# Attention and gated MLP on one core: the bias spread by a TensorE product, q of step 3 requested after W_spatial, and a new order up to the third W_spatial product

## The chip, the cores and the metric

One core of one Trainium2 chip runs the whole program. The metric is the device time of one execution in microseconds (us), and the median of several runs is what is compared. The engines are TensorE (PE, matrix products and transposes), VectorE (DVE), ScalarE (ACT), GpSimd (POOL) and SyncE (SP, which here only issues DMA requests). Each engine works through its own instructions in order and waits on semaphores for the others.

## The reference, cut to what matters

There are 4 batches of 768 tokens, 8 heads of 64 channels, and a hidden width of 1024. First comes causal linear attention with a decay per head, in blocks with a running state; the token-mixing gated MLP follows on its output.

```python
# attention, block by block of the sequence
intra = einsum('bhij,bhjd->bhid', einsum('bhic,bhjc->bhij', qb, kb) * Dmask, vb)
out[:, :, sl] = intra + einsum('bhid,bhde->bhie', qb * lam_pow, kv_state)
kv_state = lam_block * kv_state + einsum('bhsd,bhse->bhde', kb * rev_pow, vb)
# gated MLP on x = heads side by side, 512 wide
h = maximum(x @ w_in, 0);  u, v = h[..., :512], h[..., 512:]
v_n = (v - mean(v)) / sqrt(var(v) + 1e-06)
v_s = einsum('ts,bsd->btd', w_spatial, v_n) + b_spatial[None, :, None]
return (u * v_s) @ w_out
```

## The kernel before, in words

The work of one batch is three steps of 256 tokens, so there are twelve steps (0 to 11); after the three steps of a batch the spatial product and the output product of this batch follow. A step loads q, k and v (512 KB each, three buffers for each, filled in turn), multiplies q and k by decay factors, transposes both, forms the masked scores and the state, and leaves the attention output transposed in `xT`, from which the two halves of `x @ w_in` are formed.

The order of the work is written out by hand: `ORDER` is one string of tokens, read from left to right. A token is a step's name, its arguments, and the letter of the engine that runs it (T for PE, D for DVE, A for ACT, P for POOL, S for SP). Each engine runs its own tokens in the order of the string; semaphores put in by the framework let it wait for data of others and for a buffer or a PSUM bank to come free. Eight banks of PSUM are named by number as the last arguments of a token; bank 7 holds the attention state.

The names that matter here, with the line of the kernel that the profile shows:

- LQ, LK, LV (L192): load of q, k, v of a step, requested by SP. QM, KM (L280): the decay of q and k into `qc` and `kc`, in two halves. VC: v to bf16.
- TQ, TK (L310) and EQ, EK: transposes of q and k on PE and their copy out of PSUM. From step 5 on, DQ (L297) and DK (L293) do the same by a DMA transpose that SP requests.
- SC (L340): scores; MK (L345): scores times mask, on DVE; KV (L357): the state; SS: its copy to `s_sb`; AV (L378, L387): attention output in two halves, the second behind FN, a copy of one element that stands as a wait; EX: its copy to `xT`.
- WI (L243) and WS (L248): the requests for the halves of W_in and of W_spatial, issued by POOL, which converts to bf16 on the way. WO: W_out. BS (L255): the bias row, written by one DMA to all 128 partitions of `bsp`.
- PV (L412) and EV (L417, L419): the v half of `x @ w_in` and its relu; BN (L427, L428), RA (L432), RD (L437), RB (L442): mean and variance, square root, reciprocal, and the product of negated mean and reciprocal; VN (L451): the normalized v. PU (L463) and EU: the u half.
- WT (L475) and EW: transposes of W_spatial and their copies. GP: the bias into a PSUM bank; PW (L489): the W_spatial product added to it (six matmuls); GM (L495): times u. PO (L500), EO, ST: output product, copy and store.
- FL (L263): filler products of `ones` whose result nobody reads; `FL.6.256.4.0` is six of 256 columns into bank 4. GT (L239) and GN (L455): copies of one element on POOL that stand as waits, GT for a load to land, GN for a VN. tab: a load of ACT's function table.

Copies share the lines of a helper: L177 on ACT, L179 on DVE, L181 on POOL. All arguments of a token begin with the step (for GP, PW, GM, PO with the batch), so KM.3.1 is the second half of the decay of k of step 3.

Two buffers each stand behind `kc`, `qc`, `kT` and `qT`, so KM.5 can only run when KV.3.1, the last reader of step 3's `kc`, is done.

Of the kernel before, what the change touches and what calls it, by code (L numbers as in the profile page):

```python
# [562 lines left out]
```

## Time and profile before

| | us |
|---|---|
| median of 3 runs | 144.92 (144.47 to 144.94) |
| the profiled execution | 145.1 |
| its span from first to last instruction | 143.4 |
| PE busy in it | 134.0 |
| DVE busy | 111.9 |
| ACT busy | 75.9 |
| POOL busy | 57.2 |

The granted clock of PE is 1.0 over the whole execution. The profile's start is the span's start; a time in the text such as "at 19.64" is counted from there. Busy times are sums over instructions of one engine; matmuls overlap in the pipeline, so the time of a run of matmuls is best taken from the chain of waits, where each piece is counted once. A bracket at the end of a line of the timeline tells how long the engine was idle before the instruction and what ended that. Where a wait is for several things, the profile names the one that came last, and now and then it names a neighbour of it.

### The profile page before, as it was taken

The page shows a single profiled execution, that of the slowest core. Times are in us where ns is not written, and L with a number is a line of the kernel's source. Part 1 is how long each engine was busy: PE and PEld are TensorE (multiplying, and loading weights), DVE is VectorE, ACT ScalarE, POOL GpSimd, SP SyncE. Part 2 cuts the span into 40 slices and gives each one's busy share as a digit, 9 for nine tenths or more (in the row PEclk, how much of TensorE's full clock was granted, in tenths as well). Part 3 has the DMA queues.
Part 4 walks back from the last instruction along what each step waited for, and adds up shares of the span by engine and source line. Part 5 has one row for each costly group of instructions (what it writes and reads, how often), then busy time and mean ns, then how long its engine had stood idle before and what let it go on. Part 6 is the DMA issues. An engine that isn't in the chain of part 4 may idle for free.

```text
span 143.4 us, 4693 instructions
## 1 busy us (share of the span) xinstructions
PE 134.0 (93%) x1979; PEld 87.4 (61%) x1997; DVE 111.9 (78%) x222; ACT 75.9 (53%) x150; POOL 57.2 (40%) x65
## 2 busy tenths in 40 slices
PE   5998889999999999899999999999999999999990
PEld 3767655768566575566566455685664655855550
DVE  1489957899596988498999779968797989984940
ACT  3136725689726566749823567598227542580041
POOL 5657954296997514089513224603800000000000
PEclk9999999999999999999999999999999999999999
DMA  3999999999999989999989799799968251410075
GB/s 87 344 346 308 266 259 214 229 316 305 293 323 274 158 182 346 335 207 318 201 251 119 187 349 308 205 337 174 271 166 209 99 209 62 162 73 0 14 297 201
DMA packets 58374, 32.27 MB, mean 225 GB/s; under 512 B 15858, under 2 KB 55282, under 8 KB 58354
## 3 DMA queue, kind: packets, MB, share of 16 engines
q1 hardware_dynamic: 55968, 29.23, 76.8%
q0 software_dynamic: 2384, 2.75, 11.3%
q8 instruction: 15, 0.25, 0.6%
q14 instruction: 5, 0.04, 0.1%
q10 hardware_dynamic: 2, 0.00, 0.0%
HBM read 24.77 MB, written 6.29 MB: 217 GB/s over the span
## 4 chain that ended last, share of the span: by engine, by line
PE 70%; DVE 10%; DMA 5%; POOL 4%; ACT 4%; issue 2%; SPq 2%; DVEq 0%
PE ps L489 19%; PE ps L500 12%; PE ps L463 11%; PE ps L412 10%; DMA q_in<-in_q_dram 5%; PE ps L263 4%; POOL kc L280 3%; PE ps L310 3%; PE ps L340 3%; DVE a_sb L345 2%; PE ps L387 2%; PE ps L357 2%; PE ps L378 2%; SPq L293 1%; DVE wt_sb L179 1%
## 5 line engine op out<-in xcount | busy, mean ns | idle before, releaser
L489 PE MATMUL ps<-wt_sb,vn 128*128 128x384 bf16 x192 | 34.0, 327 | 0.0
L345 DVE TENSOR_TENSOR a_sb<-ps,m 128x1024 bf16<-128x1024 f32 x24 | 28.6, 1215 | 1.0 <-PE ps L340 0.6
L280 POOL TENSOR_TENSOR kc<-k_in,lv 128x512 bf16<-128x512 f32 x18 | 19.2, 1079 | 24.5 <-DMA k_in<-in_k_dram 12.1
L489 PEld LDWEIGHTS <-vn 128*128 128x128 bf16 x192 | 18.1, 98 | 12.3 <-ACT vn L448 0.4
L280 POOL TENSOR_TENSOR qc<-q_in,lqn 128x512 bf16<-128x512 f32 x19 | 20.5, 1092 | 7.7 <-DMA qT<-qc 2.8
L463 PE MATMUL ps<-xT,win_sb 128*128 128x256 bf16 x192 | 23.4, 273 | 0.0
L412 PE MATMUL ps<-win_sb,xT 128*128 128x512 bf16 x88 | 22.1, 380 | 0.6 <-DVE xT L179 0.2
L500 PE MATMUL ps<-wout_sb,gT 128*128 128x512 bf16 x82 | 21.1, 379 | 0.9 <-issue 0.6
L495 DVE TENSOR_TENSOR gT<-ps,uT 128x384 bf16<-128x384 f32 x32 | 16.8, 551 | 5.6 <-PE ps L489 4.9
L463 PEld LDWEIGHTS <-win_sb 128*128 128x128 bf16 x192 | 18.2, 98 | 3.9
L427 DVE BATCH_NORM_STATS2 st<-vh 128x6 f32<-128x512 bf16 x24 | 16.4, 682 | 1.1 <-ACT vh L417 0.7
L417 ACT ACTIVATE vh<-ps 128x512 bf16<-128x512 f32 x20 | 11.9, 596 | 9.2 <-PE ps L412 9.2
L177 ACT ACTIVATE o_sb<-ps 128x512 f32<-128x512 f32 (+1 forms) x17 | 9.6, 568 | 12.2 <-DVE o_sb L179 8.9
L412 PEld LDWEIGHTS <-xT 128*128 128x128 bf16 x96 | 8.9, 98 | 10.2 <-DVE xT L179 1.0
L500 PEld LDWEIGHTS <-gT 128*128 128x128 bf16 x92 | 8.5, 98 | 9.1 <-DVE gT L495 0.2
L177 ACT ACTIVATE ps<-bsp 128x384 f32<-128x384 f32 x21 | 10.0, 492 | 5.1 <-DVE a_sb L345 3.8
L177 ACT ACTIVATE xT<-ps 128x512 bf16<-128x512 f32 x16 | 9.1, 596 | 6.1 <-PE ps L387 6.1
L263 PE MATMUL ps<-ones 128*128 128x256 bf16 x51 | 9.2, 336 | 2.0 <-DVE ones L259 1.5
L387 PE MATMUL ps<-a_sb,vb 64*64 64x128 bf16 x384 | 10.5, 217 | 0.0
L181 POOL CAST vb<-v_in 128x1024 bf16<-128x1024 f32 x7 | 7.3, 1036 | 7.4 <-issue 5.3
L357 PEld LDWEIGHTS <-kc 64*64 64x64 bf16 x320 | 6.9, 109 | 4.2 <-issue 3.2
L417 ACT ACTIVATE uT<-ps 128x512 bf16<-128x512 f32 x16 | 9.1, 588 | 0.3 <-PE ps L463 0.3
(68 smaller groups left out, 172.8 us busy)
## 6 DMA issues: line engine op xcount, KB each, us to landing
q_in<-in_q_dram SPq DMA_DIRECT2D x12, 512.0 KB, 6.4
k_in<-in_k_dram SPq DMA_DIRECT2D x12, 512.0 KB, 6.7
v_in<-in_v_dram SPq DMA_DIRECT2D x12, 512.0 KB, 6.3
out_dram<-o_sb SPq DMA_DIRECT2D x23, 256.0 KB, 2.3
wsp_raw<-in_moe_w_spatial_dram POOLq DMA_DIRECT2D x2, 576.0 KB, 10.5
win_sb<-in_moe_w_in_dram POOLq DMA_DIRECT2D x2, 512.0 KB, 8.7
wout_sb<-in_moe_w_out_dram POOLq DMA_DIRECT2D x1, 512.0 KB, 7.8
bsp<-in_moe_b_spatial_dram SPq DMA_DIRECT2D x1, 384.0 KB, 13.4
```

The lines of the kernel that those rows point to most:

```text
L177: nc.scalar.activation(out=o, in_=i, func=AF.Copy)
L263: nc.tensor.matmul(out=bank(b)[:, 0:w], lhsT=ones[:, 0:P], rhs=ones[:, 0:w], start=(new == 1 and i == 0), stop=True, skip_group_check=True)
L280: vec(e).tensor_tensor(out=dst[n % NCA][:, u].rearrange("p u m o d -> p o (u m) d"), in0=src[n % NIN].rearrange("p (o u) m d -> p o u m d" ...
L345: nc.vector.tensor_tensor(out=a_sb[n % NA][:, i].rearrange("p o w j x -> p o w (j x)"), in0=ps[:, b0:b1 + 1:b1 - b0].rearrange("p o (w y) ...
L387: nc.tensor.matmul(out=po[c ^ o][row(w), c, i], lhsT=vb[n % NCA][row(c), 4 * o + u, j, :], rhs=a[row(c), i, o, w, j, :], start=(r == 0 and ...
L412: nc.tensor.matmul(out=bank(b), lhsT=x[:, slot(c, g)], rhs=win_sb[:, g, DH:DFF], start=(g == 0), stop=(g == NCH - 1))
L417: nc.scalar.activation(out=o, in_=i, func=AF.Relu)
L427: nc.vector.bn_stats(out=st6[p2][:, t], in_=vh[p2][:, t])
L463: nc.tensor.matmul(out=pu[:, f2].rearrange("p (c x) -> p c x", c=2), lhsT=win_sb[:, g, f * P:(f + 1) * P], rhs=x[:, slot(0, g):slot(1, g) ...
L489: nc.tensor.matmul(out=bank(b)[:, 0:HW], lhsT=vn[bb % 2][:, s, f * P:(f + 1) * P], rhs=wt_sb[:, s, i * HW:(i + 1) * HW], start=False, stop ...
L495: nc.vector.tensor_tensor(out=gT[bb % 2][:, f, cols], in0=bank(b)[:, 0:HW], in1=uT[bb % 2][:, f, cols], op=ALU.mult)
L500: nc.tensor.matmul(out=bank(b), lhsT=gT[bb % 2][:, f, t * P:(t + 1) * P], rhs=wout_sb[:, f, :], start=(f == 0), stop=(f == NCH - 1))
```

## The change

- The bias is no longer spread by DMA. A new step BR loads the row into one partition (`brow`, requested by ACT), two products BB of a row of ones with half of it (f32, 384 columns each) put it on all partitions in a PSUM bank, and two copies BE on ACT bring it to `bsp`.
- LQ.3 comes behind a new step HL on POOL: a memset of one element of the buffer that LQ.3 fills, placed right after the request for the second half of W_spatial. LK.3 and LV.3 follow LQ.3, as SP requests in order.
- Two of the three GT waits go, and RB of steps 0 to 2 with them. VN.0 goes from POOL to DVE, where the VN of steps 1 and 2 were already.
- Thirteen filler products of 256 columns in front of the first W_in product go and one of the same size comes; an earlier eight of 256 columns become sixteen of 128.
- The second table load moves from before the first state copy to before the first square root. Some copies change between ACT and DVE (EQ of step 2, EW, FN.3), and all engines' tokens up to the third W_spatial product are put in a new order; from there on the order is the same but for FN.3.4.6.

The new functions:

```diff
-    def b_sp(e):
-        nc.sync.dma_start(out=bsp, in_=moe_b_spatial.unsqueeze(0).to_broadcast((P, S)))
+    def b_r(e):
+        {"S": nc.sync, "A": nc.scalar}[e].dma_start(out=brow, in_=moe_b_spatial.unsqueeze(0))
+
+    def b_b(e, i, b):
+        nc.tensor.matmul(out=bank(b)[:, 0:HW], lhsT=one_row, rhs=brow[:, i * HW:(i + 1) * HW], start=True, stop=True)
+
+    def b_e(e, i, b):
+        copy(e, bsp[:, i * HW:(i + 1) * HW], bank(b)[:, 0:HW])
+
+    def hold(e, x, n):
+        vec(e).memset((k_in, q_in, v_in)[x][n % NIN][0:1, 0, 0, 0:1], 0.0)
```

The order, from its start to the third W_spatial product:

```diff
-msk.P one.D idn.P FL.6.256.3.1.T LQ.0.S lam.A tab.0.A row.D LK.0.S FL.2.256.2.1.T LK.1.S LB.6.T LQ.1.S
-FL.8.256.0.1.T LV.0.S LV.1.S FL.6.256.2.0.T posk.P LN.6.A LL.D LX.A QM.0.1.D QM.0.0.P KM.0.0.P KM.0.1.D
-TQ.0.0.3.T TQ.0.1.5.T EQ.0.0.3.D mkc.D TK.0.0.4.T EQ.0.1.5.A EK.0.0.4.A KM.1.0.D TK.0.1.0.T FL.4.256.1.1.T
+msk.P one.D idn.P FL.6.256.3.1.T LQ.0.S lam.A BR.A tab.0.A row.D LK.0.S FL.2.256.2.1.T LK.1.S LB.6.T LQ.1.S
+FL.16.128.0.1.T LV.0.S LV.1.S FL.6.256.2.0.T posk.P mkc.D LN.6.A LL.D LX.A QM.0.1.D QM.0.0.P KM.0.0.P KM.0.1.D
+TQ.0.0.3.T TQ.0.1.5.T EQ.0.0.3.D TK.0.0.4.T EQ.0.1.5.A EK.0.0.4.A KM.1.0.D TK.0.1.0.T FL.4.256.1.1.T
 FL.5.256.1.0.T KM.1.1.D EK.0.1.0.D GT.1.1.P LQ.2.S WI.0.P QM.1.0.D TK.1.1.1.T SC.0.0.5.6.T TK.1.0.0.T
-SC.0.1.3.4.T LK.2.S EK.1.0.0.A QM.1.1.P MK.0.0.5.6.D FL.6.256.2.0.T TQ.1.0.2.T FL.1.256.5.0.T TQ.1.1.0.T
-EQ.1.0.2.A EQ.1.1.0.A tab.1.A LV.2.S EK.1.1.1.D VC.0.P MK.0.1.3.4.D FL.6.256.1.0.T SC.1.0.0.1.T LQ.3.S
-SC.1.1.5.6.T KV.0.0.T QM.2.1.P MK.1.0.0.1.D MK.1.1.5.6.D WI.1.P SS.0.0.A AV.0.0.2.3.T FL.6.256.4.0.T VC.1.A
-FN.0.2.3.A WS.0.P KV.0.1.T AV.0.1.2.3.T TQ.2.1.4.T QM.2.0.P LK.3.S SS.0.1.D KM.2.1.P EX.0.1.3.A EX.0.0.2.D BS.S
-KV.1.0.T AV.1.0.1.6.T FN.1.1.6.D SS.1.0.A AV.1.1.1.6.T KV.1.1.T TQ.2.0.0.T SS.1.1.D EX.1.0.1.D eps.D EQ.2.0.0.D
-EQ.2.1.4.D KM.2.0.P PV.0.0.5.T PV.0.1.2.T LV.3.S TK.2.1.1.T TK.2.0.3.T EX.1.1.6.A EK.2.1.1.A EV.0.1.2.A
-EK.2.0.3.D EV.0.0.5.D PV.1.0.6.T SC.2.1.0.1.T SC.2.0.4.5.T MK.2.1.0.1.D PV.1.1.2.T EV.1.0.6.A MK.2.0.4.5.D
-EV.1.1.2.A WS.1.P VC.2.P PU.1.0.3.T PU.1.1.6.T EU.1.0.3.A GT.1.2.P LQ.4.S LK.4.S KV.2.0.T BN.0.0.D AV.2.0.0.1.T
-SS.2.0.A FN.2.0.1.A BN.0.1.D RA.0.A AV.2.1.0.1.T RD.0.D RB.0.D EX.2.1.1.A EU.1.1.6.A PU.0.1.2.T EX.2.0.0.D
-BN.1.0.D VN.0.0.P VN.0.1.P BN.1.1.D EU.0.1.2.A PV.2.0.5.T EV.2.0.5.A RA.1.A PV.2.1.4.T EV.2.1.4.A QM.3.1.P
-QM.3.0.P WT.0.0.3.T WT.1.0.6.T PU.0.0.5.T WT.2.0.2.T EW.0.0.3.A PU.2.0.3.T BN.2.0.D RD.1.D RB.1.D BN.2.1.D
-RA.2.A EW.1.0.6.A EW.2.0.2.D EU.0.0.5.A WT.2.1.1.T PU.2.1.0.T WT.1.1.2.T WT.0.1.6.T RD.2.D RB.2.D EU.2.0.3.A
-GT.2.1.P LV.4.S LQ.5.S LK.5.S VN.1.0.D VN.1.1.D GP.0.0.0.4.A EU.2.1.0.A VN.2.0.D VN.2.1.D GN.2.1.P KM.3.1.P
-KM.3.0.P EW.2.1.1.D PW.0.0.0.4.T EW.0.1.6.D EW.1.1.2.A TQ.3.2.6.T GP.0.2.0.5.A PW.0.2.0.5.T TK.3.2.1.T
-GM.0.0.0.4.D EK.3.2.1.D GP.0.3.1.3.A EQ.3.2.6.A PW.0.3.1.3.T GP.0.1.0.0.A VC.3.P KM.4.0.P GM.0.2.0.5.D
+SC.0.1.3.4.T LK.2.S EK.1.0.0.A QM.1.1.P MK.0.0.5.6.D FL.6.256.2.0.T TQ.1.0.2.T TQ.1.1.0.T EQ.1.0.2.A EQ.1.1.0.A
+LV.2.S EK.1.1.1.D VC.0.P MK.0.1.3.4.D BB.1.2.T BE.1.2.A FL.1.256.1.0.T SC.1.0.0.1.T SC.1.1.5.6.T KV.0.0.T
+QM.2.1.P MK.1.0.0.1.D MK.1.1.5.6.D WI.1.P AV.0.0.2.3.T FN.0.2.3.A SS.0.0.A VC.1.A BB.0.4.T WS.0.P KV.0.1.T
+AV.0.1.2.3.T BE.0.4.A TQ.2.1.0.T QM.2.0.P SS.0.1.D KM.2.1.P EX.0.1.3.A EX.0.0.2.D KV.1.0.T AV.1.0.1.6.T
+FN.1.1.6.D TQ.2.0.4.T SS.1.0.A AV.1.1.1.6.T KV.1.1.T SS.1.1.D EX.1.0.1.D eps.D EX.1.1.6.A EQ.2.1.0.A EQ.2.0.4.A
+KM.2.0.P PV.0.0.5.T EV.0.0.5.D PV.0.1.2.T EV.0.1.2.A PV.1.0.6.T BN.0.0.D BN.0.1.D TK.2.1.1.T EK.2.1.1.A
+TK.2.0.3.T EK.2.0.3.D EV.1.0.6.A PV.1.1.2.T SC.2.1.0.1.T SC.2.0.4.5.T MK.2.1.0.1.D EV.1.1.2.A tab.1.A
+MK.2.0.4.5.D RA.0.A WS.1.P HL.1.3.P LQ.3.S LK.3.S LV.3.S VC.2.P PU.1.0.3.T PU.1.1.6.T EU.1.0.3.A EU.1.1.6.A
+LQ.4.S LK.4.S KV.2.0.T RD.0.D BN.1.0.D BN.1.1.D AV.2.0.0.1.T SS.2.0.A FN.2.0.1.A RA.1.A PU.0.1.2.T AV.2.1.0.1.T
+VN.0.0.D EX.2.1.1.A EU.0.1.2.A EX.2.0.0.D VN.0.1.D WT.0.0.3.T WT.1.0.6.T EW.0.0.3.D RD.1.D VN.1.0.D VN.1.1.D
+PV.2.0.5.T EV.2.0.5.A BN.2.0.D PV.2.1.4.T EV.2.1.4.A EW.1.0.6.A BN.2.1.D QM.3.1.P QM.3.0.P WT.2.0.2.T EW.2.0.2.D
+PU.0.0.5.T EU.0.0.5.A RA.2.A PU.2.0.3.T WT.2.1.1.T EW.2.1.1.D GP.0.0.0.4.A PU.2.1.0.T EU.2.0.3.A WT.1.1.2.T
+WT.0.1.6.T RD.2.D VN.2.0.D VN.2.1.D LV.4.S LQ.5.S LK.5.S EU.2.1.0.A GN.2.1.P KM.3.1.P KM.3.0.P PW.0.0.0.4.T
+EW.0.1.6.D EW.1.1.2.D GP.0.2.0.5.A GP.0.3.1.3.A TQ.3.2.6.T PW.0.2.0.5.T TK.3.2.1.T GM.0.0.0.4.D EK.3.2.1.D
+EQ.3.2.6.A PW.0.3.1.3.T GP.0.1.0.0.A VC.3.P KM.4.0.P GM.0.2.0.5.D
...
```

More of the change, by code (lines that the diff above doesn't have):

```diff
@@ new lines @@
+GP.0.3.0.4.A QM.4.0.P QM.4.1.P KV.3.0.T MK.3.0.5.6.D LV.5.S MK.3.1.1.2.D PW.0.3.0.4.T GM.0.3.0.4.D SS.3.0.D
+PW.0.1.0.0.T GP.0.0.1.5.A GP.0.1.1.3.A KM.4.1.P WO.P TQ.4.2.6.T VC.4.P EQ.4.2.6.A PW.0.1.1.3.T TK.4.2.1.T
+EK.4.2.1.A GM.0.1.1.3.D PW.0.0.1.5.T GM.0.1.0.0.D LK.6.S QM.5.1.P GM.0.0.1.5.D QM.5.0.D AV.3.0.4.6.T
+SC.4.1.0.1.T KV.3.1.T FN.3.4.6.A KM.5.0.P KM.5.1.P SC.4.0.2.3.T GP.0.2.1.5.A AV.3.1.4.6.T MK.4.1.0.1.D DQ.5.S
+PW.0.2.1.5.T EX.3.0.4.A EX.3.1.6.A PV.3.0.1.T EV.3.0.1.A MK.4.0.2.3.D DK.5.S GM.0.2.1.5.D LV.6.S PV.3.1.0.T
@@ new lines @@
+PU.3.0.2.T EV.3.1.0.A SS.3.1.D KV.4.0.T AV.4.0.0.3.T SS.4.0.A EU.3.0.2.A FN.4.0.3.A LQ.8.S LQ.6.S LK.7.S
+BN.3.0.D VC.5.D BN.3.1.D PO.0.5.4.T RA.3.A KV.4.1.T EO.0.5.4.D AV.4.1.0.3.T SS.4.1.A KM.6.0.P SC.5.0.5.6.T
+KM.6.1.P LQ.7.S DK.6.S SC.5.1.1.2.T EX.4.1.3.D EX.4.0.0.A KV.5.0.T PO.0.2.4.T VC.6.A SS.5.0.A PV.4.0.3.T
+PV.4.1.0.T RD.3.D MK.5.1.1.2.D RB.3.D KV.6.0.T EV.4.1.0.A SS.6.0.A EO.0.2.4.A EV.4.0.3.A MK.5.0.5.6.D
+AV.5.0.1.6.T PO.0.4.2.T KV.6.1.T KM.7.0.P KM.7.1.P VN.3.1.A QM.6.0.P FN.5.1.6.D AV.5.1.1.6.T PU.4.1.0.T QM.6.1.D
@@ new lines @@
+LK.8.S EX.5.0.1.D EX.5.1.6.A QM.7.1.P QM.7.0.P LV.7.S PV.5.1.6.T PV.5.0.4.T PO.0.0.5.T EV.5.1.6.A EO.0.4.2.D
+BN.4.1.D PU.5.1.6.T PU.3.1.1.T GP.1.2.1.3.D LK.9.S DQ.6.S BN.4.0.D RA.4.A BN.5.1.D EU.4.1.0.D EV.5.0.4.A
+GP.1.0.1.2.A VN.3.0.A EU.3.1.1.A EO.0.0.5.A RD.4.D RB.4.D SS.6.1.D BN.5.0.D KM.8.1.P VC.7.P DQ.7.S GP.1.2.0.5.A
+RA.5.A RD.5.D VN.4.1.D RB.5.D QM.8.0.P PU.4.0.0.T EU.4.0.0.A QM.8.1.P VN.5.1.D VN.4.0.A PO.0.1.4.T PU.5.0.1.T
+PO.0.3.0.T VN.5.0.A EU.5.1.6.A PW.1.2.0.5.T EO.0.3.0.A KM.8.0.D GP.1.1.1.6.A PW.1.2.1.3.T DK.7.S GM.1.2.0.5.D
@@ new lines @@
+PW.1.1.1.6.T EO.0.1.4.A GP.1.3.1.0.D EU.5.0.1.D GM.1.2.1.3.D PW.1.0.1.2.T LV.9.S GM.1.1.1.6.D GP.1.0.0.1.D
+GM.1.0.1.2.D KV.7.0.T SC.6.1.3.4.T LV.8.S SC.6.0.5.6.T MK.6.1.3.4.D PW.1.0.0.1.T PW.1.3.1.0.T DK.8.S
+MK.6.0.5.6.D SS.7.0.A GP.1.3.0.4.A PW.1.3.0.4.T GM.1.0.0.1.D GM.1.3.1.0.D AV.6.0.2.3.T GM.1.3.0.4.D FN.6.2.3.A
+GP.1.1.0.4.D SC.7.1.0.1.T SC.7.0.5.6.T KV.7.1.T AV.6.1.2.3.T DQ.8.S SS.7.1.A PW.1.1.0.4.T EX.6.0.2.A EX.6.1.3.A
+PV.6.0.2.T LQ.10.S MK.7.1.0.1.D KM.9.1.P GM.1.1.0.4.D KM.9.0.D PO.1.1.1.T PO.1.0.0.T PO.1.4.4.T EO.1.1.1.A
@@ new lines @@
+EV.6.0.2.A EO.1.0.0.A VC.8.P PO.1.5.3.T LK.10.S LQ.9.S ST.0.1.S MK.7.0.5.6.D EO.1.4.4.A BN.6.0.D KV.8.0.T
+AV.7.0.0.5.T EO.1.5.3.A SC.8.0.1.2.T SC.8.1.3.4.T SS.8.0.D FN.7.0.5.D ST.1.5.S AV.7.1.0.5.T ST.0.3.S PO.1.2.6.T
+EX.7.1.5.A EX.7.0.0.A PV.7.1.5.T PV.6.1.0.T MK.8.0.1.2.D QM.10.0.D MK.8.1.3.4.D VC.9.P EV.7.1.5.A BN.7.1.D
+PV.7.0.2.T ST.0.2.S QM.9.0.P DK.9.S QM.9.1.P QM.10.1.P EV.6.1.0.A BN.6.1.D GP.2.3.1.5.A KV.9.0.T AV.8.0.1.3.T
+KM.10.1.P EV.7.0.2.A PU.6.1.0.T SS.9.0.D FN.8.1.3.D KV.9.1.T EO.1.2.6.A AV.8.1.1.3.T RA.6.A BN.7.0.D RD.6.D
@@ new lines @@
+EX.8.1.3.D ST.1.4.S LV.10.S LQ.11.S LK.11.S DQ.9.S PU.6.0.2.T GP.2.2.0.6.D RB.6.D VN.6.0.D DQ.10.S ST.0.4.S
+RA.7.A RD.7.D KM.10.0.D EX.8.0.1.A EU.6.1.0.A PV.8.1.1.T EV.8.1.1.A RB.7.D BN.8.1.D PV.8.0.4.T EV.8.0.4.A
+BN.8.0.D VN.7.1.A EU.6.0.2.A VN.6.1.A VN.7.0.D DK.10.S RA.8.A PU.8.0.0.T PU.7.1.3.T PU.8.1.1.T EU.7.1.3.A
+PU.7.0.2.T RD.8.D RB.8.D GP.2.0.0.4.D VN.8.0.D VN.8.1.A PW.2.2.0.6.T GM.2.2.0.6.D PW.2.0.0.4.T EU.7.0.2.A
+EU.8.1.1.A KM.11.1.P QM.11.1.P EU.8.0.0.D KM.11.0.P QM.11.0.P GM.2.0.0.4.D ST.1.0.S LV.11.S VC.10.D GP.2.0.1.3.A
@@ new lines @@
+PW.2.0.1.3.T PW.2.3.1.5.T GM.2.0.1.3.D GP.2.1.0.0.A GP.2.3.0.6.A SS.9.1.A PW.2.1.0.0.T GM.2.3.1.5.D GP.2.1.1.3.A
+GM.2.1.0.0.D KV.10.0.T SC.9.1.1.2.T MK.9.1.1.2.D SC.9.0.4.5.T SS.10.0.A PW.2.1.1.3.T DK.11.S PW.2.3.0.6.T
+MK.9.0.4.5.D PO.1.3.2.T GM.2.3.0.6.D GM.2.1.1.3.D AV.9.0.0.1.T EO.1.3.2.D SC.10.0.4.5.T KV.10.1.T FN.9.0.1.A
+AV.9.1.0.1.T EX.9.1.1.A MK.10.0.4.5.D DQ.11.S SC.10.1.2.3.T VC.11.A GP.2.2.1.5.A PO.2.2.6.T EX.9.0.0.D
+PV.9.1.4.T PV.9.0.1.T ST.0.0.S ST.1.3.S MK.10.1.2.3.D PW.2.2.1.5.T EV.9.1.4.D EO.2.2.6.A SS.10.1.A ST.2.2.S
@@ new lines @@
+BN.11.1.D PU.9.0.2.T EU.9.0.2.D PU.10.0.4.T PU.11.0.1.T ST.2.0.S ST.1.2.S RA.10.A RD.10.D RB.10.D RA.11.A
+RD.11.D EU.10.1.3.D RB.11.D VN.9.1.A GP.3.0.0.2.A EO.2.5.5.A GP.3.2.0.3.A VN.11.0.A VN.11.1.A ST.1.1.S ST.2.5.S
+PU.11.1.0.T PO.2.4.5.T EO.2.4.5.A EU.11.0.1.D VN.10.0.D VN.10.1.D PW.3.2.1.6.T PW.3.0.0.2.T GP.3.1.1.1.D
+EU.11.1.0.D GP.3.1.0.5.D PW.3.1.0.5.T GP.3.3.0.0.D EU.10.0.4.A GM.3.0.0.2.D PW.3.3.0.0.T PW.3.2.0.3.T
+GP.3.0.1.4.D GM.3.2.0.3.D GP.3.3.1.3.D GM.3.1.0.5.D PW.3.0.1.4.T PW.3.1.1.1.T GM.3.3.0.0.D PO.3.0.2.T
@@ L85 @@
+PW.3.3.1.3.T PO.3.2.5.T GM.3.1.1.1.D EO.3.0.2.D GM.3.0.1.4.D GM.3.2.1.6.D GM.3.3.1.3.D ST.3.0.S ST.2.4.S
+EO.3.2.5.D PO.3.4.2.T EO.3.4.2.A ST.3.2.S ST.3.4.S PO.3.1.3.T PO.3.3.6.T EO.3.1.3.D ST.3.1.S PH.3.5.0.3.T
+EO.3.3.6.A PH.3.5.1.5.T ST.3.3.S EH.3.5.0.3.A SH.3.5.0.S FL.1.256.0.0.T EH.3.5.1.5.A SH.3.5.1.S
 """
@@ L152 @@
     bsp = sb([P, S], FP32, "bsp")
+    brow = sb([1, S], FP32, "brow")
     ones = sb([P, 512], BF16, "ones")
@@ L523, in st_o @@
         eng.dma_start(out=out[bb, t * P:(t + 1) * P, :], in_=o_sb[(bb * NT + t) % NO])
-    ops = dict(GT=after, GN=after_vn, one=c_ones, FL=f_l, FN=f_n, lam=c_lam, posk=c_posk, tab=c_tab, row=c_row, eps=c_eps, LB=l_b, LN=l_n, LL=l_l, LX=l_x, idn=c_ident, msk=c_mask, mkc=c_mask2, WI=w_in, WS=w_sp, WO=w_out, BS=b_sp,
+    ops = dict(GT=after, GN=after_vn, one=c_ones, FL=f_l, FN=f_n, lam=c_lam, posk=c_posk, tab=c_tab, row=c_row, eps=c_eps, LB=l_b, LN=l_n, LL=l_l, LX=l_x, idn=c_ident, msk=c_mask, mkc=c_mask2, WI=w_in, WS=w_sp, WO=w_out, BR=b_r, BB=b_b, BE=b_e, HL=hold,
                LK=ld_k, LQ=ld_q, LV=ld_v, KM=k_m, QM=q_m, DK=d_k, DQ=d_q, VC=v_c, TK=t_k, TQ=t_q, EK=e_k, EQ=e_q,
```

55 lines of the change are left out of this document (6 added, 49 removed).

## The prediction

> **What bounds the kernel now.** First the page: engines and the chain that ended last.
>
> ```profile
> PE 134.0 (93%) x1979; PEld 87.4 (61%) x1997; DVE 111.9 (78%) x222; ACT 75.9 (53%) x150; POOL 57.2 (40%) x65
> PE 70%; DVE 10%; DMA 5%; POOL 4%; ACT 4%; issue 2%; SPq 2%; DVEq 0%
> ```
>
> TensorE (PE) is the bound, so a change pays only where it closes a PE gap or takes PE work away. Then the windows of 5 us (busy PE, PEld, DVE, ACT, POOL, then clock, DMA share, GB/s):
>
> ```profile
> 10.00:15.00 5.00, 4.50 (x126) 3.67 (x125) 4.70 (x5) 3.10 (x5) 4.00 (x4) 1.00 1.19 303
> 15.00:20.00 5.00, 4.17 (x136) 3.16 (x135) 3.41 (x7) 2.92 (x6) 3.17 (x5) 1.00 1.17 279
> 20.00:25.00 5.00, 4.74 (x57) 2.65 (x57) 3.62 (x8) 1.92 (x4) 3.13 (x4) 1.00 1.18 216
> 30.00:35.00 5.00, 5.00 (x61) 4.38 (x60) 4.54 (x14) 4.47 (x10) 4.36 (x5) 1.00 1.12 346
> 35.00:40.00 5.00, 4.52 (x53) 2.88 (x54) 3.39 (x8) 3.71 (x7) 4.32 (x6) 1.00 0.98 286
> 40.00:45.00 5.00, 5.00 (x86) 3.60 (x79) 4.16 (x7) 2.27 (x4) 4.99 (x6) 1.00 1.08 316
> ```
>
> PE has gaps up to 40 us and hardly any after; the stretch that the change reorders ends at 39.4, with the third W_spatial product. Next the chain of waits in order of time: does a gain at 40 us reach the end?
>
> ```profile
> 44.70 1.01 POOL qc L280
> 45.71 0.72 issue
> 46.43 2.27 POOL kc L280 x2
> 48.70 0.05 issue
> 48.80 1.94 SPq L293
> ...
> 52.07 7.46 DMA q_in<-in_q_dram
> 59.58 0.04 issue
> 59.62 0.69 DVE qc L280
> ```
>
> It should. KM.5 at 46.43 needs KV.3.1 of PE (kc has two buffers); DK.5 needs KM.5; LQ.6 stands behind DK.5 in SP's order; its q releases DVE at 59.6, and from 61 us the chain is PE almost alone. PE is full from 40 to 45, so what it gains by 39.8 moves KV.3.1 and all behind it one for one. Last, the timeline of the stretch (start, us, engine):
>
> ```profile
> 12.57 4.59 SPq L192 DMA_DIRECT2D q_in<-in_q_dram  x1
> 19.64 2.04 POOL L280 TENSOR_TENSOR kc<-k_in,lv 128x512 bf16<-128x512 f32 x2 [1.82 <-PE ps L310]
> 20.60 7.59 SPq L255 DMA_DIRECT2D bsp<-in_moe_b_spatial_dram  x1
> 32.20 2.04 POOL L280 TENSOR_TENSOR qc<-q_in,lqn 128x512 bf16<-128x512 f32 x2
> 33.30 0.96 DVE L442 SCALAR_TENSOR_TENSOR nmr<-mv,rstd 128x2 f32<-128x2 f32 x1
> 35.19 1.14 PE L489 MATMUL ps<-wt_sb,vn 128*128 128x384 bf16 x6
> 39.81 0.64 PE L340 MATMUL ps<-qT,kT 64*64 64x128 bf16 x32 [0.27 <-DVE gT L495]
> ```
>
> SP hangs 7.59 us on the bias request, and LV.3, LQ.4, LK.4 stand behind it. From the tile views (issue plus landing): first W_in half 9.73+8.7=18.4, second 23.9, W_spatial 27.5 and 31.2, q of step 3 12.57+19.0=31.6, its k 33.1. W_spatial is first used at 30.3 and 33.2: nobody waits for it. Holding q back is worth nothing by itself; it only covers the earlier WT, and its price comes under the rivals. KM.2 at 19.64 is marked as waiting for TQ.2.0, but stands ahead of it in the order, so it waits for step 2's k to land: the change leaves that load alone, so TK.2 stays at about 21.7.
>
> **The change part by part**, as a walk along PE. Prices from the chain: PV (4 matmuls) 0.86, PU (8) 0.87, PW (6) 0.97, WT (6) 0.33, eight transposes 0.45, a step's SC 0.45, KV 0.28, half an AV about 0.46.
>
> *Start to the first PV.* Thirteen filler matmuls of 256 columns go and one comes: 12 x 0.14 = 1.7 us of PE time, one of them (bank 5) now waiting 0.47 for MK.0.0. FL.8.256 becoming FL.16.128 keeps the columns and adds eight weight loads, 0 to 0.8 us; I take 0.2, hidden since QM.1.0 on DVE runs 9.86 to 11.36 in any case. The brow request on ACT costs about 0.5 before the first table load, which ends 1.3 us before LN.6 needs it. The mask copies (0.44) move off KM.1.0's way, but KM.1.0 waits for its k: nothing. The sqrt table load (1.28) leaves ACT at 13.68, but SS.0.0 now stands behind FN.0 and so behind AV.0.0: 14.98 becomes about 14.85. BB, one row in f32 by 384 columns, is not in this trace: below, two passes at PW's 0.16 each, 0.32; above, four times that, 1.30. The row of its kind (L212, two matmuls for one product) shows the passes but only 8 columns; I take the middle, 0.65. BB.1.2 lies in the wait for EQ.1.1.0 (12.75 to 13.4), BB.0.4 in the wait for SS.0.0 (14.6 to 15.2); at 1.30 SC.1 slips 0.6, but the first PV only 0.1. BE costs ACT 0.49 twice, ahead of EX.0.1, no later than before. MK.1.0 starts near 14.0 (14.25), KV.1.0 after SS.0.1 at 16.8, and TQ.2.0 goes before AV.1.1 as soon as QM.2.0 ends (17.82). First PV: 18.9 instead of 19.42, gain 0.5. The floor is the W_in landing, 18.4.
>
> *First PV to first PW.* Work: 6 PV 5.16, 6 PU 5.22, 6 WT 2.0, TK.2 and SC.2 0.95, KV.2 and AV.2 1.2: 14.5 us. Before it took 15.77, so 1.27 were gaps (KM.2, MK.2, SS.2.0). After: PV.1.0 and PV.1.1 lie over KM.2 and the eviction of TK.2; PU.1.0 then waits for the second W_in half at 23.9, 0.5; MK.2 ends at 25.55 (25.83); SS.2.0 comes at 27.0 to 27.2 on ACT, behind the table load (now 24.1 to 25.4) and two EU, with PU.0.1 as cover until 27.3. WT.0.0 and WT.1.0 cover EX.2. Gaps 0.9, first PW at 34.3 instead of 35.19: gain 0.4 in this stage. On DVE VN.0 joins (POOL needed 4.14 for the pair, DVE's rows give 0.34 each) with two EW (0.5 each); two EQ (0.42 each) and three RB (0.16, 0.16, 0.96) go. EQ.2 on ACT is 0.6 each, less two EW of 0.8. At no price: HL, one memset of 0.1 on POOL, and the two GT copies that go (the second held LV.4 on SP until 34.39).
>
> *First PW to SC.3.0.* Before 4.62 for 3.8 of work; the gaps were EW.0.1.6 (about 0.35), KM.3, and GM.0.2 behind EK.3 (0.4). After, EW.0.1.6 ends before PW.0.0.0 does, and KM.3 starts with GN.2.1 at 34.4 (35.82), so only the 0.4 stays: SC.3.0 at 38.5, gain 0.4. FN.3.4.6 goes to an idle ACT. The bias rows (384 KB, at 300 GB/s 1.3 us of DMA) free the loads of steps 3 to 5, which keeps POOL's row up to QM.5.1 fed; PE is full there, no further gain.
>
> *Against it.* VN.1 and VN.2 (DVE, near 29.6 and 33.5) have QM.3 on POOL close by. The nmr row shows the price: 0.96 instead of 0.16 while POOL's qc ran, until that ended at 34.24. [...] From the rows: one VN kept waiting loses 0.8 to 1.04 on DVE, of which TQ.3 has some 0.5 of slack; I charge 0.35.
>
> Sum: 0.5 + 0.4 + 0.4 - 0.35 = 0.95. The profiled execution took 145.1 (span 143.4), so it would be 144.15; it lies 0.2 over the median of 144.92, which becomes **144.0**.
>
> **Rivals.** (1) *The gaps close further*: PV at 18.5, second W_in half half a microsecond earlier as LQ.3 no longer shares the DMA engines, no collision: 0.4 + 0.5 + 0.35 more, 142.7. For it: W_in's transfers run at 216 GB/s with q and k beside them. Against: MK.1 on DVE still sets KV.1.0. [...] (3) *q of step 3 comes too late*, the slower side. HL stands behind WS.1 on POOL (21.6 + 0.8), so LQ.3 goes out at 22.5 instead of 12.57 and shares the DMA with W_spatial; behind it on SP's queue stand LK.3, LV.3 and all loads up to LK.6, and QM.3 and KM.3 on POOL wait for them. From landing at T come QM.3 2.1, GN, KM.3 2.05 and waiting, TK.3 at T+5.1; before it was 37.95, so it decides from T = 32.85. A load in a free queue takes 6.4 to 8.2 (30.7); those beside the weights took 15.8 and 19.0 (41.5). I estimate 30.5, as the weights are through at about 29.5; at W_spatial's own 11.5 T is 34.0 and the kernel loses 1.15: 146.1. (4) *W_spatial's hold does nothing*: as worked out, it is in no term of the sum, so this is the forecast.
>
> **How the numbers follow.** A measurement here can tell about 0.3%, 0.43 us. Forecast (gain 0.43 to 1.5) 0.50; (1) 0.14; (2) 0.16; (3), with the table load's delay of SS.2.0 in small, 0.20. Faster 0.64, same 0.16, slower 0.20. The range from 142.8 to 145.7 reaches into (1) and into the mild half of (3) and leaves about 0.1 out on either side.
>
> **What would show it.** Right: first PV near 18.9, first PW near 34.3, SC.3.0 near 38.5, q of step 6 landing near 58.6, PE packed from 60. Wrong: QM.3 starting after 33, VN rows of 1 us or more, SC.3.0 not earlier than 39.4, or a gain at 40 us that a new wait between 46 and 60 swallows.

## The result, and the profile after

| | before | after |
|---|---|---|
| median, both on the same chip (19 executions each) | 144.91 us (144.4 to 145.88) | 144.49 us (143.5 to 146.83) |
| ratio after to before | | 0.9953, interval 0.993 to 0.9976 |
| the profiled execution (its span) | 145.1 (143.4) | 143.63 (141.9) |

The kernel is 0.5% faster, some 0.7 us by the ratio. Three executions of the kernel after, at a mean granted clock of 0.976 to 0.988, take 145.9 to 146.8 us; the median counts them and the ratio does not. The two profiled executions lie 1.47 us apart, twice the ratio: the one of after is 0.86 below its median, the one of before 0.2 above. So sizes in the following are read between stages, not summed from the two spans.

The page of the kernel after, first engines, then the chain that ended last:

```profile
PE 132.8 (94%) x1980; PEld 86.7 (61%) x1997; DVE 110.6 (78%) x220; ACT 76.2 (54%) x153; POOL 53.5 (38%) x62
PE 72%; DMA 14%; DVE 4%; SPq 3%; ACT 2%; issue 1%; POOL 0%; DVEq 0%; ACTq 0%
```

PE lost 1.2 us of busy time, 0.5 of it ahead of the first PV, where 12 fillers went (1.7 us at 0.14 each) and two BB came (0.84 each to the start of the next matmul); the rest is spread over the span. In the chain DVE fell from 10% to 4% and the DMA engines rose from 5% to 14%, with the landing of W_in alone at 7%. The windows of 5 us of the kernel after (busy PE, PEld, DVE, ACT, POOL, then clock, DMA share, GB/s):

```profile
15.00:20.00 5.00, 3.99 (x132) 2.72 (x133) 3.61 (x7) 3.74 (x9) 3.94 (x6) 1.00 1.20 244
20.00:25.00 5.00, 5.00 (x63) 2.98 (x63) 3.68 (x9) 3.36 (x6) 2.66 (x4) 1.00 1.20 209
30.00:35.00 5.00, 5.00 (x54) 4.17 (x53) 4.24 (x11) 4.11 (x9) 2.07 (x3) 1.00 1.02 289
35.00:40.00 5.00, 4.73 (x84) 3.27 (x82) 3.51 (x7) 2.59 (x5) 5.00 (x6) 1.00 1.10 330
```

From 15 to 20 PE is idle for a whole microsecond, more than before (0.83); from 20 on it is nearly full. The chain of waits of the kernel after says what ends that idle time:

```profile
9.49 0.68 POOL seen L239
10.17 9.32 DMA win_sb<-in_moe_w_in_dram
19.48 0.04 issue
19.53 0.38 PE ps L421
...
28.08 0.30 DVE vn L460
28.40 0.70 DVE xT L179
29.10 0.27 issue
29.38 1.67 PE ps L421 x7
...
48.01 1.67 SPq L302
49.73 4.65 DMA v_in<-in_v_dram
```

The first W_in half decides when the first PV may start, and its request waited on POOL for GT.1.1. At 29.1 us PE waits once more, 0.27, for DVE's half of EX.2. (That half stands behind VN.0, but this costs it little: ACT starts the other half at 28.36, DVE its own at 28.40.) At the end the old link from the loads of step 6 is there still, with v as its load now. The timeline of the stretch, kernel after (start, us, engine):

```profile
9.49 0.73 POOL L239 COPY seen<-q_in 1x1 f32<-1x1 f32 x1 [1.42 <-DMA q_in<-in_q_dram]
9.50 0.68 DVE L289 TENSOR_TENSOR qc<-q_in,lqn 128x512 bf16<-128x512 f32 x1
10.17 0.94 POOL L243 DMA_DIRECT2D win_sb<-in_moe_w_in_dram  x1
12.65 0.91 PE L258 MATMUL ps<-brow,one_row 1*128 1x384 f32 x2
18.84 2.04 POOL L289 TENSOR_TENSOR kc<-k_in,lv 128x512 bf16<-128x512 f32 x2 [1.05 <-PE ps L396]
19.53 2.75 PE L421 MATMUL ps<-win_sb,xT 128*128 128x512 bf16 x11 [0.57 <-DMA win_sb<-in_moe_w_in_dram]
31.28 2.04 POOL L289 TENSOR_TENSOR qc<-q_in,lqn 128x512 bf16<-128x512 f32 x2 [6.19 <-DMA q_in<-in_q_dram]
34.85 1.14 PE L498 MATMUL ps<-wt_sb,vn 128*128 128x384 bf16 x6
39.10 0.64 PE L349 MATMUL ps<-qT,kT 64*64 64x128 bf16 x32 [0.27 <-DVE gT L504]
```

The first three of these instructions (GT.1.1, QM.1.0 and the request for W_in) stood like this in the kernel before:

```profile
9.61 0.18 POOL L239 COPY seen<-q_in 1x1 f32<-1x1 f32 x1 [1.70 <-DMA q_in<-in_q_dram]
9.73 0.97 POOL L243 DMA_DIRECT2D win_sb<-in_moe_w_in_dram  x1
9.86 1.50 DVE L280 TENSOR_TENSOR qc<-q_in,lqn 128x512 bf16<-128x512 f32 x1
```

The milestones in the two profiles: first PV 19.42 before, 19.53 after; first PW 35.19 and 34.85; SC.3.0 39.81 and 39.10; the request of DQ.5 47.37 and 46.25. So 0.7 us is won by SC.3.0, and another 0.4 between 40 and 47 us, where nothing in the order changed but FN.3.4.6. One pair of profiles gives such sizes only roughly: the kernel before with FN.3 alone moved (an experiment below, the same order up to 45 us) has its first PV at 19.16 and SC.3.0 at 39.66 (39.39 in another execution). Against it the new order loses 0.4 to the first PV and wins 0.3 to 0.6 by SC.3.0.

### The profile page after: what moved, and what is told of

Same layout as the page of the kernel before. It is cut to its first block, busy times and chain, and to the rows that moved or that the text cites. A ratio compares the mean times of both kernels' runs of the same rounds, so it can differ in the third digit from the quotient of the medians.

```text
span 141.9 us, 4688 instructions
## 1 busy us (share of the span) xinstructions
PE 132.8 (94%) x1980; PEld 86.7 (61%) x1997; DVE 110.6 (78%) x220; ACT 76.2 (54%) x153; POOL 53.5 (38%) x62
## 4 chain that ended last, share of the span: by engine, by line
PE 72%; DMA 14%; DVE 4%; SPq 3%; ACT 2%; issue 1%; POOL 0%; DVEq 0%; ACTq 0%
PE ps L498 21%; PE ps L472 13%; PE ps L509 13%; PE ps L421 13%; DMA win_sb<-in_moe_w_in_dram 7%; DMA q_in<-in_q_dram 4%; DMA v_in<-in_v_dram 3%; PE ps L349 3%; PE ps L396 3%; PE ps L366 3%; DVE a_sb L354 2%; SPq L192 2%; PE ps L319 2%; PE ps L387 1%; SPq L302 1%
## 5 line engine op out<-in xcount | busy, mean ns | idle before, releaser
L289 POOL TENSOR_TENSOR qc<-q_in,lqn 128x512 bf16<-128x512 f32 x19 | 20.0, 1069 | 14.2 <-DMA q_in<-in_q_dram 8.5
L181 POOL CAST vb<-v_in 128x1024 bf16<-128x1024 f32 x7 | 7.8, 1118 | 8.1 <-issue 5.3
L366 PE MATMUL ps<-vb,kc 64*64 64x64 bf16 x320 | 8.6, 194 | 0.4 <-DVE s_sb L179 0.3
```

Of the source, the lines that this page charges most:

```text
L289: vec(e).tensor_tensor(out=dst[n % NCA][:, u].rearrange("p u m o d -> p o (u m) d"), in0=src[n % NIN].rearrange("p (o u) m d -> p o u m d" ...
L366: nc.tensor.matmul(out=pkv[row(o), u], lhsT=kc[n % NCA][row(c), u, m, o, :], rhs=vb[n % NCA][row(c), 4 * o + u, m, :], start=new and u == ...
```

## The experiments

Each ratio is to the kernel before on the same chip. "The new order" is the order of the kernel after.

**The kernel after, unchanged, a second time.** Is GT's 0.73 chance?

> The changed kernel once more, as the measure for its variants on this chip and for a second profile. Mine: 144.2 to 144.5, ratio to before 0.994 to 0.997; the one-element wait on POOL (GT.1.1) takes 0.7 us beside DVE's q of step 1 again, so that W_in's first half goes out near 10.2 and the first W_in product waits until 19.4 to 19.6; SC.3.0 near 39.1. Rival, that this was chance in one execution: GT.1.1 takes 0.2, W_in lands near 18.5, the first product starts at 18.9 to 19.0 and SC.3.0 at 38.5.

Measured: 0.9947 (0.9912 to 0.9982). In its profile GT.1.1 takes 0.73 again, W_in is requested at 10.08, the first PV starts at 19.46 and SC.3.0 at 39.03. The late request belongs to the order.

**Without the hold.**

```diff
-MK.2.0.4.5.D RA.0.A WS.1.P HL.1.3.P LQ.3.S LK.3.S LV.3.S
+MK.2.0.4.5.D RA.0.A WS.1.P LQ.3.S LK.3.S LV.3.S
```

> The changed kernel without HL: q, k and v of step 3 are requested as soon as the ring has room (near 12.5), all else as it is. Mine (the hold is in no term of the sum): the same as the changed kernel within 0.3 us; W_spatial lands 1.5 to 2 us later (near 31 to 32), q of step 3 near 31, the transposes of W_spatial wait at most 0.3 us. Rival (the hold is what makes the new order work): W_spatial's first half lands after 28.2, where its transposes start, and the second after 33; 0.5 to 1.5 us lost, as slow as before or slower.

Measured: 0.998 (0.9946 to 1.0013). The waits of PE in its profile (engine, line, what it waited for, us in total, times, longest):

```profile
PE ps L468 <- DMA win_sb<-in_moe_w_in_dram: 0.8, 1, 0.8
PE ps L480 <- DMA wsp_raw<-in_moe_w_spatial_dram: 0.2, 1, 0.2
```

Without the hold the second half of W_in lands at 24.70 instead of 23.70, and PU waits 0.8 for it; the first PW starts at 35.34 and SC.3.0 at 39.60, 0.5 later than in the kernel after. The intervals of the two ratios overlap, so the 0.3% between them is not proven by the times; the wait in the profile shows how it could come about.

**The masks late.** If QM.1.0 on DVE doesn't start while GT.1.1 is due, GT is short again.

```diff
-posk.P mkc.D LN.6.A
+posk.P LN.6.A
-EK.0.1.0.D GT.1.1.P
+EK.0.1.0.D mkc.D GT.1.1.P
```

> The changed kernel with the two mask copies (mkc, 0.44 us on DVE) behind EK.0.1.0, so that DVE's q of step 1 is ready 0.4 us later than POOL's GT.1.1 and W_in's request. [...]

Measured: 148.93 us median (145.41 to 149.44, 6 executions; five of them at a mean granted clock of 0.965 to 0.977), with no ratio for that reason. In the profile, an execution of 145.41, the row of GT:

```profile
9.51 0.26 POOL L235 COPY seen<-q_in 1x1 f32<-1x1 f32 x1 [1.41 <-DMA q_in<-in_q_dram]
```

that of QM.1.0:

```profile
10.82 2.45 DVE L285 TENSOR_TENSOR qc<-q_in,lqn 128x512 bf16<-128x512 f32 x1
```

and the largest wait of PE:

```profile
PE ps L315 <- DVE qc L285: 1.6, 1, 1.6
```

GT takes 0.26, W_in is requested at 9.72 and landed at 17.75: GT was short once QM.1.0 didn't start beside it. But now it is DVE that loses. While POOL goes from its request at 9.72 through QM.1.1 and VC.0 to 12.7, the two mask copies take 1.27 (0.55 in the kernel after) and QM.1.0 takes 2.45, against 0.68 in the kernel after and 1.50 in the kernel before; PE waits 1.6 for it in front of TQ.1.0, and the first PV starts at 20.49. The repair costs more than the fault.

**FN.3 alone**, in the kernel before.

```diff
-FN.3.4.6.D
+FN.3.4.6.A
```

> The kernel before with one token changed: FN.3.4.6 on ACT instead of DVE. Mine now (AV.3.1 waited 0.26 us for that copy, which stood behind DVE's q of step 5): AV.3.1 right behind the work ahead of it, DQ.5 about 0.4 us earlier, total 0.3 to 0.5 us faster than before (144.4 to 144.6). The prediction's pricing (nothing): the same as before within 0.15 us.

Measured: 0.9964 (0.9931 to 0.9997). SC.3.0 at 39.66, DQ.5 at 46.80 (47.37 in the kernel before): by this measurement one token gives most of the gain. The timelines show why, first the kernel before:

```profile
46.11 0.68 DVE L280 TENSOR_TENSOR qc<-q_in,lqn 128x512 bf16<-128x512 f32 x1
46.71 0.14 DVE L179 COPY seen<-ps 1x1 f32<-1x1 f32 x1
46.90 0.31 PE L378 MATMUL ps<-qT,s_sb 64*64 64x128 bf16 x8 [0.26 <-DVE seen L179]
```

and then the kernel after:

```profile
45.28 0.16 ACT L177 ACTIVATE seen<-ps 1x1 f32<-1x1 f32 x1 [0.31 <-PE ps L396]
45.67 0.22 PE L387 MATMUL ps<-qT,s_sb 64*64 64x128 bf16 x2
```

On DVE the copy that stands as a wait was queued behind QM.5.0, and PE waited 0.26 for it with the second half of AV.3; on ACT it is done before PE asks. The price repeats in every profile of this study: from SC.3.0 to the request of DQ.5 it takes 7.56 and 7.55 us in the two kernels with FN.3 on DVE, and 7.14 or 7.15 in eleven of the twelve profiles with FN.3 on ACT (7.26 in the twelfth, the bias by DMA).

**FN.3 back on DVE in the kernel after.**

```diff
-FN.3.4.6.A
+FN.3.4.6.D
```

> The changed kernel with one token back: FN.3.4.6 on DVE as before. Mine now (that token is more than half of the gain): AV.3.1 waits 0.2 to 0.3 us for the copy again, and the time is 0.4 to 0.6 us above the changed kernel, ratio to before 0.998 to 1.000. Rival (the prediction's account: the new order up to the third W_spatial product gives the gain, FN.3 nothing): ratio to before 0.994 to 0.996, within 0.2 us of the changed kernel.

Measured: 0.9991 (0.9969 to 1.0013). The wait is back, in the timeline of this kernel:

```profile
46.38 0.14 DVE L175 COPY seen<-ps 1x1 f32<-1x1 f32 x1
46.57 0.31 PE L383 MATMUL ps<-qT,s_sb 64*64 64x128 bf16 x8 [0.25 <-DVE seen L175]
```

All the rest of the change together, without this token, is worth 0.1%, at most 0.3% by the interval, which can't be told from nothing.

**The fillers back** in the new order: six ahead of SC.1 instead of one, six ahead of BB.0.4, four ahead of the first PV.

```diff
-FL.1.256.1.0.T SC.1.0.0.1.T
+FL.6.256.1.0.T SC.1.0.0.1.T
-BB.0.4.T
+FL.6.256.4.0.T BB.0.4.T
-PV.0.0.5.T
+FL.4.256.5.0.T PV.0.0.5.T
```

> The changed kernel with fillers in three places where PE waits: six of 256 columns ahead of SC.1 (instead of one), six ahead of BB.0.4, four ahead of the first W_in product, which waits for its weights. Mine (the removed fillers are also what keeps the granted clock up; in the changed kernel some executions had a mean clock of 0.976 and took 2 to 3 us more, in the kernel before none): mean clock 0.995 or more in all runs, the undisturbed time within 0.3 us of the changed kernel, the median over all runs 0.2 to 0.4 us lower. Rival 1 (fillers are plain PE work on the path): 0.5 to 1.5 us slower. Rival 2 (the clock has nothing to do with the fillers): the same share of runs near 0.976.

Measured: 0.9999 (0.9974 to 1.0025); first PV at 20.00, SC.3.0 at 39.74, and a mean granted clock of 0.995 or more in all 12 executions. The fillers do cost time, 0.5% against the kernel after, though PE waits in that stretch anyway (rival 1); and the clock stays up with them, as expected.

**The bias by DMA in the new order**, requested behind LK.3 as the old order had it.

```diff
-BR.A, BB.1.2.T BE.1.2.A, BB.0.4.T BE.0.4.A
-LQ.3.S LK.3.S LV.3.S
+LQ.3.S LK.3.S BS.S LV.3.S
```

> The changed kernel with the bias spread by DMA as before (requested between k and v of step 3) instead of by two TensorE products and two copies. Mine (384 KB more for the DMA engines ahead of v of step 3 and the loads of step 4): v of step 3 and q, k of step 4 land 1 to 1.5 us later, but PE is full there and waits for none of them; within 0.3 us of the changed kernel; BB gone saves PE 2 x 0.6 us in places where it waits anyway. Rival (the bias's DMA time is what the change wins): 0.7 to 1.3 us slower than the changed kernel, QM.4 or VC.3 on POOL starting 1 us later and TQ.4 waiting. If the copies of the bias into PSUM wait for its landing, the first W_spatial product starts after 35.5 and it is slower than before.

Measured: 1.0017 (0.999 to 1.0044), 0.7% over the kernel after. The SP rows of its timeline:

```profile
23.81 5.36 SPq L251 DMA_DIRECT2D bsp<-in_moe_b_spatial_dram  x1
29.22 0.43 SPq L188 DMA_DIRECT2D v_in<-in_v_dram  x1
29.75 1.96 SPq L188 DMA_DIRECT2D q_in<-in_q_dram  x1
```

With the hold, the row's request falls among the loads that POOL needs next: LV.3 goes out at 29.22 instead of 22.83 and LQ.4 at 29.75 instead of 27.82. The size is the rival's, but the profile doesn't show its path. PE's largest waits in it are 0.8 for the first W_in half and 0.8 for VC.2, behind v of step 2, a load requested before the row; and two kernels without the row have that load as late (the two with fillers; see the last section). The profiled execution took 146.09, 0.9 over its kernel's median. So the edit costs 0.7%, and by which wait stays open.

**Masks late and fillers back together.** How much of the loss of the late masks was clock?

```diff
-posk.P mkc.D
+posk.P
+EK.0.1.0.D mkc.D
-FL.6.256.2.0.T TQ.1.0.2.T
+FL.16.256.2.0.T TQ.1.0.2.T
```

and the fillers as above.

> The kernel of e3 (mask copies late, W_in requested 0.4 us earlier), with fillers where PE waits: ten more ahead of TQ.1.0 and the three places of e6. Mine (e3's 148.9 us came of PE's clock, 0.965 on the mean, after PE had waited 1.6 us for DVE's q of step 1): mean clock 0.995 or more, 144.2 to 145.2 us. Rival (e3 is slow for the late q of step 1 itself, whatever the clock): 147 us or more with the clock at 0.995.

Measured: 1.0144 (1.0105 to 1.0183), 146.45 us; first PV at 21.74, SC.3.0 at 41.32; clock 0.993 to 0.996 but for one execution. So some 2.5 us of the 148.93 was clock; 2 us over the kernel after stay by the medians (1.9% by the ratios). The late q of step 1 and the fillers themselves would explain them, but which takes how much was not separated.

**Fillers only where PE waits.**

```diff
-TK.0.0.4.T
+FL.6.256.2.0.T TK.0.0.4.T
-PV.0.0.5.T
+FL.4.256.5.0.T PV.0.0.5.T
```

> The new order with two groups of fillers put where PE waits anyway: six of 256 columns (0.84 us by 0.14 each) ahead of TK.0.0, where PE waits 0.89 for POOL's kc at 7.24, and four (0.56) ahead of the first PV, where PE waits 0.6 for the W_in landing. Theory: in a wait a filler costs nothing, and it keeps PE's granted clock up: first PV within 0.2 of 19.5, the undisturbed time within 0.3 us of the new order's 144.35, and the mean granted clock 0.99 or more in at least 10 of 12 executions, where the new order showed it in 21 of 31. Rival 1: it is the fillers between 13 and 17 us, which do cost time, that keep the clock: then it is below 0.99 in 3 or more of 12. Rival 2: the fillers run past the waits and delay TK.0.0 and PV.0: first PV at 19.9 or later and 0.3 to 0.6 us slower than the new order.

Measured: 1.0038 (1.001 to 1.0067), and a mean granted clock below 0.99 in 4 of 12 executions. The first PV starts at 19.52, as without them: they cost nothing there, and they don't keep the clock up, so it is the fillers between 13 and 16 us that do (rival 1). That they don't delay the first PV but the kernel is still 0.9% over the kernel after was in no expectation. The chain of waits of its profile shows where its time went:

```profile
10.82 14.54 DMA v_in<-in_v_dram
25.38 0.04 POOLq L178
25.43 0.08 issue
25.51 1.05 POOL vb L178
26.55 0.04 issue
26.60 0.38 PE ps L363 x13
```

v of step 2 was complete at 25.36 here. In the kernel after its last part landed at 23.91 and VC.2 started at 24.06, early enough for PE. Here PE loses 0.6 at KV.2, and the first PW comes at 35.34. Why the load was later, with the same request time, isn't shown; more of it below.

**FN.3 alone, again.**

> The kernel before with FN.3.4.6 on ACT and nothing else, a second time, beside the two kernels that add to it. It was 0.9964 [0.9931, 0.9997] of the time before. Theory: again 0.995 to 0.998, some 0.4 to 0.6 us, and PW.0.2.1 and DQ.5 0.4 to 0.6 earlier than before. Rival: the first comparison was at the edge of its interval, and the move is worth 0.1% or less (0.999 to 1.001).

Measured: 0.9975 (0.9954 to 0.9996). Two measurements, both below 1 with their whole interval.

**FN.3 and the bias by PE in the old order.**

```diff
-BS.S
+lam.A BR.A
+MK.0.1.3.4.D BB.1.2.T BE.1.2.A
+FL.6.256.4.0.T BB.0.4.T
+AV.0.1.2.3.T BE.0.4.A
-FN.3.4.6.D
+FN.3.4.6.A
```

> The kernel before with FN.3.4.6 on ACT and the bias row spread by PE (BR, BB, BE) in the old order, with the old fillers, waits and loads. Theory: what the bias by PE gains in the new order (1.0 us against the DMA) is there in the old order too, since the 7.59 us of SP's request and the 384 KB go in both: 0.5 to 1.0 us under the kernel with FN.3 alone, 143.3 to 143.8, with LV.3, LQ.4 and LK.4 landing 1 us earlier or more. Rival: in the old order nobody waits for those loads, and the two products cost PE 0.9 each way between 12 and 16 us: equal to the kernel with FN.3 alone within 0.3 us, or up to 0.9 slower.

Measured: 1.0084 (1.0051 to 1.0116), 1.1% over FN.3 alone. The timeline of PE:

```profile
12.83 0.91 PE L255 MATMUL ps<-brow,one_row 1*128 1x384 f32 x2
13.67 0.83 PE L269 MATMUL ps<-ones 128*128 128x256 bf16 x6
14.43 0.64 PE L346 MATMUL ps<-qT,kT 64*64 64x128 bf16 x32
...
16.48 0.91 PE L255 MATMUL ps<-brow,one_row 1*128 1x384 f32 x2
17.32 0.34 PE L363 MATMUL ps<-vb,kc 64*64 64x64 bf16 x10
```

SC.1 starts at 14.43 (13.40 with FN.3 alone) and the first PV at 20.40 (19.16): both products lie on the path when the fillers stay, and the loads that go out earlier have nobody waiting. SC.3.0 at 40.42 against 39.66. The whole loss against FN.3 alone, 1.1% or 1.6 us, is nearly twice the rival's upper end, and half of it lies behind this stretch: from the request of DQ.5 to the end of the span this profile takes 96.83, that of FN.3 alone 95.60. What makes that half isn't shown.

**The same with the hold.**

```diff
-LQ.3.S, LK.3.S, LV.3.S
+WS.1.P HL.1.3.P LQ.3.S LK.3.S LV.3.S
```

> The kernel with FN.3.4.6 on ACT and the bias by PE in the old order, and LQ.3, LK.3 and LV.3 behind HL after W_spatial's second request. Theory: the hold lets the second half of W_in land 0.3 to 0.9 earlier, as it did in the new order: the first PU and the first PW 0.3 to 0.5 earlier and the time 0.3 to 0.5 us under the kernel without it. Rival 1: in the old order PU comes late enough to hide that landing: within 0.2 us. Rival 2: q of step 3 lands after 31.5 and KM.3 and TK.3 with it: up to 0.5 us slower.

Measured: 1.0085 (1.0053 to 1.0117): nothing. The second half of W_in lands 0.62 earlier (23.41 against 24.03), and the first PU starts at 24.95, long after either: rival 1.

Together: the kernel before with FN.3 alone has ratios of 0.9964 and 0.9975, the kernel after 0.9953 and 0.9947, and the intervals overlap (the medians are the other way round, 144.19 and 144.36 against 144.49 and 144.47, as those of the kernel after hold its executions at a lower clock). Whether the rest of the change adds anything to FN.3 is not shown. Within the new order the missing fillers are worth 0.5% and the bias by PE 0.7%, and the hold 0.3%, which is not beyond the intervals; in the old order the bias by PE costs 1.1% and the hold nothing. The parts pay for one another, and what they leave is about 0.1%. Part of these losses lies far behind the stretch: from the request of DQ.5 to the end the kernel after takes 95.65, the fillers back 96.41 and the fillers in the waits 96.56, and in these two PE waits 0.6 near 97 us for a VN. Why is open.

## Why the prediction was right, and where its steps were not

The time, 144.49 for a forecast of 144.0 with a range of 142.8 to 145.7, and the sign were right. The sum's 0.95 compares with 0.7 by the ratio. But its largest term failed, and a term it priced at nothing took its place. That the number came so near is in good part luck: the loss of the first stage and the 0.35 that wasn't paid cancel, and of the 0.7 the token without a price makes 0.4 to 0.5, while all that the sum priced is worth 0.1% with that token taken back. The path that it gave, through KM.5, is there in the pair of profiles (46.43 before, 45.72 after, the 0.7 of SC.3.0), but how much of that reaches the end isn't shown.

*Start to the first PV, gain 0.5 (18.9).* Wrong: 19.53, a loss of 0.1. The term that failed is the floor, "the W_in landing, 18.4", taken over from before with its request at 9.73. The request moved to 10.17, since GT.1.1 went from 0.18 to 0.73, and the landing to 19.48. (That is 1.0 later for a request 0.44 later; why the transfer itself took 9.3 instead of 8.7 isn't shown.) Without PE's wait of 0.57 for it the first PV would stand at 18.96, as forecast. GT met QM.1.0: before, GT finished in 0.18 and DVE's QM.1.0 took 1.50 beside POOL; after, KM.1 starts 0.36 earlier on DVE (7.95), QM.1.0 starts together with GT (within 0.02 us in all the profiles of the new order but the two with late masks), takes 0.68, and it is POOL that loses. I had put such a meeting of DVE and POOL into the sum for VN and QM.3 alone. GT, from 9.49 for 0.73, ends 0.04 after QM.1.0, from 9.50 for 0.68; which was first can't be read from starts 0.01 apart, and by what the one holds up the other isn't shown. With the late masks the loss is on the other side: GT 0.26, QM.1.0 2.45. "The mask copies move off KM.1.0's way: nothing" was the edit whose price this was. Besides, k of step 2 landed at 18.68 instead of 19.48, so KM.2 started at 18.84, where I had left it "alone" at 19.64. That isn't shown to come of the late W_in: with the late masks, where W_in went out early, it landed at 18.72, and over the profiles anywhere from 17.7 to 19.7.

*BB, 0.65 each, bounds 0.32 and 1.30.* Measured 0.91 for one product by its row, 0.84 to the start of the next matmul: inside the bounds and above the middle. In the new order it took the place of six fillers (0.82), and SC.1 starts at 13.71 against 13.72. In the old order it came on top of them.

*First PV to first PW, gain 0.4.* The size was right, 0.45 (15.32 against 15.77); the gaps were others. The wait of 0.5 for the second W_in half never came, as it landed at 23.70 and PU starts at 24.09. In its place PE waited 0.27 for EX.2, which WT.0.0 and WT.1.0 didn't cover to the end.

*First PW to SC.3.0, gain 0.4.* Right: 4.25 against 4.62, 0.37.

*VN beside QM.3, 0.35 against.* Not paid where I put it. VN.1 takes 0.73 for its pair at 29.99, VN.2 0.74 at 34.17, and QM.3 runs from 31.28 to 33.32, clear of both. No run shows the 0.35; where the two did meet, with the masks late, VN.1's pair took 2.11 from 30.96, and QM.3 2.09 from 30.83 (2.04 in the kernel after), so the loss of 1.38 was on DVE. In the kernel after it was GT that lost, 0.55.

*"FN.3.4.6 goes to an idle ACT", no price.* The missed term. I named the engine that it goes to, and not what it left: on DVE it stood behind QM.5.0, and PE behind it. By the two ratios it is worth 0.25 to 0.36%, 0.4 to 0.5 us, the only part of the change that won time when it was measured by itself.

*The hold, "worth nothing by itself".* Wrong in the new order by its profile: 0.5 us, by the second W_in half, the very term that I had put into rival 1 only (the times give 0.3%, within the intervals). In the old order it is indeed worth nothing.

*Fillers, 1.7 us of PE time.* I took them for covered; back in the new order they cost 0.5% (SC.3.0 39.74 against 39.10). And they have a use that I didn't mention, the clock.

*The rivals.* Rival 1's W_in term was real against the new order without the hold (23.70 for 24.70), but only 0.2 against the kernel before (23.87), and GT's delay kept the first PV from 18.5. Rival 2, that QM.3 meets both VN pairs and the time stays at 144.8, is outside the interval. Rival 3 was decided as I set it: q of step 3 landed at 31.21 (estimate 30.5), short of 32.85, and QM.3 started at 31.28. Rival 4, that the hold does nothing, was in the forecast; the profile without the hold speaks against it, the times don't decide. Of the signs that I named, the first PV missed, the first PW at 34.85 stood halfway, SC.3.0 at 39.10 stayed under 39.4, and step 6's q landed at 57.97, before 58.6, on FN.3's account.

## What to carry to other kernels

When a one-element copy stands as a wait, ask what is queued ahead of it on its engine: moving one such token off a busy engine won 0.25 to 0.36%, where the whole rewritten order with it won 0.5%. When an edit starts a VectorE instruction earlier, look at what GpSimd is about to do at that moment, above all at a DMA request behind it, and measure both: here GT.1.1 took 0.73 beside QM.1.0 for 0.18 ahead of it, and the request for W_in went out 0.44 later. And test the parts of a change both in the old order and in the new: the bias by PE is worth 0.7% in the one and costs 1.1% in the other.
